# Decay attention and gated convolution on one core: first loads in halves, one more unit of 512-column value products, another hand-written order

## The chip, the cores and the metric

The kernel runs on one core of one Trainium2 chip. The metric is the device time of one execution in microseconds (us), the median of several runs. The engines are PE (TensorE, matrix products; PEld is its loading of weights), DVE (VectorE), ACT (ScalarE), POOL (GpSimd) and SP (SyncE, which here only issues transfers). All transfers go through one queue that SP feeds, onto 16 DMA engines.

## The reference

Four batches, eight heads, 768 positions and head dimension 64. A causal attention with decay and without softmax, computed block by block with a running state, is followed by a layer over 512 channels: a depthwise convolution of five taps gives a gate, a product with `w_val` gives a value, and gate times value goes through `w_out`.

```python
for b in range(nb):                       # blocks of 64 positions
    intra = einsum('bhic,bhjc->bhij', qb, kb) * Dmask      # lam ** (i - j), lower triangle
    intra = einsum('bhij,bhjd->bhid', intra, vb)
    inter = einsum('bhid,bhde->bhie', qb * lam_pow, kv_state)
    out[:, :, sl] = intra + inter
    kv_state = lam_block * kv_state + einsum('bhsd,bhse->bhde', kb * rev_pow, vb)
...
gate = sigmoid(sum_k conv_w[k] * x_shifted[k])             # five taps
result = (gate * (x @ w_val)) @ w_out
```

`w_val`, `w_out` and `conv_w` arrive as 64-bit floats.

## The kernel before

The work is cut into 12 chunks of 128 positions, each for two batches: six chunks for one pair of batches, then six for the other. For each chunk i there are, on PE, the scores `s.i` (k times q), the products `ia.i` (masked scores times v), `in.i` (q times state) and `st.i` (k times v, for the state). `ia` and `in` add up in the PSUM tile `xp`. In the first three chunks (`BIG`) the scores come in two halves, `s.i.0` into the tile `s` and `s.i.1` into `so`, and the products work on whole chunks; in the others they work on 64 x 64 tiles (`s.i.0` then holds all heads). DVE masks the scores (`m.i.b.u`, tile `A`) and updates the state (`up`); POOL scales q (`qd`) and lets the state fade (`fd`); ACT or POOL scales k (`kd`, written into the loaded tile `lv`); ACT copies `xp` away (`x`) and splits it into two float32r parts (`xh`; the low part `xl` on DVE or POOL).

Two chunks make a unit. A unit goes through the convolution (`t.un.ct.kk`, first tap on ACT, four on DVE, then `sg`, the sigmoid) and the value product with `w_val`. Each product with a weight is three matmuls (high times high, low times high, high times low), over four tiles of channels: 12 matmuls for a piece. A value piece is `v.i.f` for one chunk (256 columns) or `V.un.f` for a whole unit (512 columns), the latter for the units in `WIDE`. Gate times value is `ap`, its split `hh` and `hl`, the product with `w_out` is `p.i.b.j.u`, its copy `ev` and its store `o`. The weights are widened from 64 bits by seven small steps on DVE and ACT and one on POOL (`wv.u.k.*`, `wo.u.k.*`, `cv.*`).

SP issues loads in halves of a chunk: `ld.i.0` holds q and k with heads on partitions (tile `lq`, 1 MB), `ld.i.2` holds v and k with positions on partitions (tile `lv`, 1 MB); a half of a weight is 1 MB as well. The PSUM tile `s` has one buffer, so the scores of the next chunk wait for both masks of the chunk before.

Each engine works through its queue in order. What stands in each queue is decided by one text, `ORDER`: a list of all pieces, each with the buffers it takes after a colon. `Plan.run` walks through it and records piece after piece. The kernel begins with nine warming matmuls (`warm`), and `f.0` is one filling matmul.

Of the kernel before, what the change touches and what calls it, by code (L numbers as in the profile page):

```python
# [36 lines left out]
fd.0.0 kd.1.0 wo.1:hs1 m.1.1.1 wv.0.1.n ia.1.0:xp0 ia.1.1 wv.0.1.m:u2 ld.4.2:lv0 wv.1.0.e:val2 in.1.0 st.1:u0 wv.0.1.s
wv.0.1.w wv.0.1.v wv.0.1.h ld.3.2:lv1 wv.1.0.n s.2.0:s0 wv.1.1.e:val3 s.2.1:u1,u2 up.1.0 xh.1 wv.0.1.l v.0.1
m.2.0.0:A0 m.2.1.0 wv.1.0.m:u0 xl.1 wv.1.0.w wv.1.0.r hi.0 pb.0.0:val0 m.2.0.1:A1 wv.1.0.s cv.e qd.2.0:qd1 wv.1.0.v
qd.2.1 wv.1.1.n x.1 wv.1.1.r cv.r s.4.0:s0 cv.n v.1.0:u3 v.1.1 wv.1.0.h wv.1.1.s wv.1.1.m:u0 m.2.1.1 wv.1.1.w wv.1.1.v  # L40
ia.2.0:xp0 ia.2.1 wv.1.0.l cv.m m.4.1.0:A0 kd.2.0 wv.1.1.h fd.1.0 wo.0.0.n:val1 cv.s in.2.0 x.2:x1 pb.1.0:val2
wv.1.1.l m.4.0.0 st.2:u1 wo.0.0.e wo.0.0.r up.2.0 qd.4.0:qd0 cv.w cv.v xh.2:xs1 wo.1.1.e:val3 t.0.0.0:u2,g0 s.3.0:s0
xl.2.0 wo.0.0.m:u0 v.0.2:u3 m.3.0.0:A1 ld.6.2:lv2 v.0.3 pb.0.1 t.0.0.1 kd.3.0 t.0.0.2 xl.2.1 t.0.0.3 wo.0.0.w qd.4.1
ld.5.0:lq2 wo.0.0.s t.0.0.4 v.1.2:u1 sg.0.0 qd.3.1:qd1 v.1.3 v.2.2:u3 v.2.3 pb.1.1 wo.1.1.n fd.2.0 wo.0.0.v m.3.1.0
wo.1.1.m:u2 wo.1.1.r ld.6.0:lq0 st.3:u0,u1 wo.0.0.h qd.3.0 ia.3.0:xp0 in.3.0 wo.1.1.w wo.1.1.s wo.1.1.v wo.0.0.l hi.1
s.5.0:s0 kd.4.0 v.2.0:u2 up.3.0 in.3.1 wo.0.1.e:val1 wo.0.1.r fd.3.0 wo.1.1.h wo.0.1.n wo.0.1.m:u0 wo.0.1.s wo.1.1.l
up.3.1 fd.3.1 ia.3.1 v.2.1 x.3 xh.3 xl.3.1 ia.4.0:xp0 t.0.1.0:u1 ld.5.2:lv1 wo.0.1.w xl.3.0 pb.2.0:val3 m.5.1.0:A1
m.5.0.0 wo.0.1.v pb.2.1 wo.0.1.h wo.0.1.l s.6.0:s0 st.4:u0,u2 qd.5.1:qd1 kd.6.0 t.0.1.1 t.0.1.2 t.0.1.3 in.4.0 up.4.0
fd.4.0 t.0.1.4 sg.0.1 v.3.0:u3 kd.5.0 v.3.2:u0 qd.5.0 in.4.1 ia.4.1 ld.7.2:lv0 t.0.3.0:u1 t.0.3.1 up.4.1 t.0.3.2
x.4:x2 t.0.3.3 t.0.2.0:u2 kd.5.1 v.3.3 pb.3.1:val1 t.0.2.1 t.0.2.2 xh.4:xs0 ld.7.0:lq1 ia.5.0:xp0 in.5.0 t.0.2.3  # L50
fd.4.1 st.5:u0 up.5.0 v.3.1 pb.3.0 t.0.3.4 xl.4.1 in.5.1 sg.0.3 t.0.2.4 ap.1.0 ap.0.0 sg.0.2 ap.1.1 xl.4.0
wo.1.0.e:val2 wo.1.0.r v.4.0:u0 v.4.2:u3 wo.1.0.n wo.1.0.m:u1 ap.0.1 v.4.1 wo.1.0.s hh.1.1:hs0 wo.1.0.w pb.4.0:val0
hh.1.0 hl.1.1 wo.1.0.v m.6.1.0:A0 v.4.3 m.6.0.0 t.1.1.0:u2,g1 t.1.1.1 wo.1.0.h ia.5.1 st.6:u0,u1 up.6.0 x.5 s.7.0:s0
ia.6.0:xp0 hl.1.0 p.1.1.0.0:u0 t.1.1.2 hh.0.1:hs1 hh.0.0 t.1.1.3 pk.6 wo.1.0.l p.1.1.0.1 pb.4.1 qd.6.1:qd0 t.1.1.4
qd.6.0 t.1.3.0:u3 sg.1.1 t.1.3.1 t.1.3.2 t.1.3.3 t.1.3.4 ev.1.1.0:o0 o.1.1.0 xh.5 in.6.1 hi.2 ia.6.1 p.1.0.0.0:u2
fd.6.0 x.6:x0 t.1.0.0:u0 hl.0.0 sg.1.3 hl.0.1 p.1.0.0.1 up.6.1 ld.11.2:lv1 t.1.0.1 t.1.0.2 t.1.0.3 t.1.0.4
p.0.1.0.0:u1 ev.1.0.0:o1 p.0.1.0.1 t.1.2.0:u3 m.7.0.0:A1 t.1.2.1 t.1.2.2 t.1.2.3 m.7.1.0 sg.1.0 xl.5.0 p.0.0.0.0:u2
p.0.0.0.1 xl.5.1 v.5.0:u0 ld.8.0:lq2 t.1.2.4 ev.0.1.0:o2 o.1.0.0 xh.6:xs1 qd.7.0:qd1 t.2.3.0:u1,g0 v.5.1 ap.3.0
ld.8.2:lv2 ev.0.0.0:o0 sg.1.2 pb.5.0:val2 ap.3.1 ap.2.0 qd.7.1 kd.7.1 ia.7.0:xp0 in.7.0 kd.7.0 ap.2.1 hh.2.1:hs0
st.7:u2,u3 fd.6.1 v.5.2:u0 v.5.3 hh.2.0 t.2.3.1 t.2.3.2 up.7.0 s.8.0:s0 in.7.1 t.2.3.3 t.2.1.0:u2 t.2.3.4 hh.3.0:hs1  # L60
ia.7.1 hh.3.1 hl.2.0 sg.2.3 pb.5.1 p.2.0.0.0:u1 t.2.0.0:u0 t.2.1.1 ld.9.2:lv0 t.2.1.2 t.2.0.1 fd.7.0 up.7.1 hl.2.1
# [841 lines left out]
```

## Time and profile before

| | |
|---|---|
| median of 3 runs | 206.36 us (206.08 to 206.38) |
| profiled execution, own time | 206.52 us |
| span of its profile | 204.7 us |
| PE busy | 197.6 us, 97% of the span |
| DVE busy | 154.1 us, 75% |
| ACT, POOL busy | 114.3 and 115.4 us, 56% each |
| granted TensorE clock | 1.00 of full speed throughout |
| read, written | 29.38 MB, 6.29 MB |

The profile lists what each engine did from the start of the span; idle time carries what ended it. The own time of the profiled execution is 1.8 us longer than the span. PE is busy for nearly the whole span, so the places to read are those where PE waits and what the waiting pieces wait for.

### The profile page before, as it was taken

To read this page: it belongs to the slowest core of one execution; us is meant where nothing else is said; L and a number is where in the kernel's file an instruction comes from. 1 tells how busy PE (TensorE), PEld (TensorE's weight loads), DVE (VectorE), ACT (ScalarE), POOL (GpSimd) and SP (SyncE) were. 2 spreads that over 40 slices of the span, in tenths; PEclk is the share of its full clock that TensorE was granted. 3 is DMA by queue.
4 is the path that set the end of the run, shared out by engine and by line. 5 is a ranking of instruction groups with operands and counts; after the bars stand their busy time and mean duration, and the time that the engine had idled before them with its cause. 6 is when DMAs were issued, how large, how long until landed. Compare 5 with 4: busy or idle time off the path is not lost.

```text
span 204.7 us, 7451 instructions
## 1 busy us (share of the span) xinstructions
PE 197.6 (97%) x3312; PEld 171.6 (84%) x3312; DVE 154.1 (75%) x240; ACT 114.3 (56%) x218; POOL 115.4 (56%) x113
## 2 busy tenths in 40 slices
...
GB/s 175 426 429 419 422 424 423 421 360 27 195 51 362 8 3 118 373 232 3 297 297 29 203 400 122 3 3 152 8 106 0 0 3 102 102 51 14 93 127 78
DMA packets 7952, 36.15 MB, mean 177 GB/s; under 512 B 1136, under 2 KB 1392, under 8 KB 4336
## 3 DMA queue, kind: packets, MB, share of 16 engines
...
q14 instruction: 6, 0.05, 0.1%
HBM read 29.38 MB, written 6.29 MB: 174 GB/s over the span
## 4 chain that ended last, share of the span: by engine, by line
PE 87%; DMA 9%; SPq 2%; issue 0%; ACT 0%; ACTq 0%
PE op L841 33%; PE vp L732 33%; DMA lq<-in_qkv 9%; PE xp L510 5%; PE s L470 5%; PE xp L547 5%; PE st L572 4%; SPq L337 1%; PE xp L525 1%; PE s L460 1%; PE st L564 1%; PE xp L536 1%; SPq L355 0%; PE so L460 0%; ACT o L848 0%
## 5 line engine op out<-in xcount | busy, mean ns | idle before, releaser
L706 DVE SCALAR_TENSOR_TENSOR acc<-x,conv_sb,acc 128x512 f32<-128x512 f32 x96 | 71.5, 753 | 7.8 <-ACT acc L704 5.7
L732 PE MATMUL vp<-x_hi,wv_hi 128*128 128x256 f32 (+1 forms) x144 | 47.1, 327 | 0.0
L732 PE MATMUL vp<-x_hi,wv_lo 128*128 128x256 f32 (+1 forms) x144 | 45.9, 319 | 0.3 <-POOL wv_lo L303 0.3
L732 PE MATMUL vp<-x_lo,wv_hi 128*128 128x256 f32 (+1 forms) x144 | 45.8, 318 | 0.0
L841 PE MATMUL op<-wo_hi,hs 128*128 128x512 f32 x96 | 30.4, 398 | 0.0
L848 ACT COPY o<-op 128x512 f32<-128x512 f32 (+1 forms) x25 | 14.3, 570 | 28.5 <-PE op L841 24.2
L732 PEld LDWEIGHTS vp<-x_hi,wv_hi 128*128 128x128 f32 x144 | 27.3, 190 | 2.8
L732 PEld LDWEIGHTS vp<-x_hi,wv_lo 128*128 128x128 f32 x144 | 27.4, 190 | 2.4 <-POOL wv_lo L303 0.5
L732 PEld LDWEIGHTS vp<-x_lo,wv_hi 128*128 128x128 f32 x144 | 27.4, 190 | 1.9
L677 POOL TENSOR_TENSOR x_lo<-x,x_hi 128x512 fp32r<-128x512 f32 x20 | 25.8, 1311 | 4.7 <-ACT x_hi L666 4.7
L584 POOL TENSOR_TENSOR sdec<-state,qdec_c 128x512 f32<-128x512 f32 x17 | 18.4, 1080 | 9.2 <-DVE state L581 9.2
L814 POOL TENSOR_TENSOR hs<-g,hs 128x512 fp32r<-128x512 f32 x12 | 15.4, 1294 | 13.6 <-ACT hs L803 13.6
L420 POOL TENSOR_TENSOR qd<-lq,qdec_c 128x512 f32<-128x512 f32 (+1 forms) x18 | 22.6, 1272 | 0.0
L841 PEld LDWEIGHTS op<-wo_hi,hs 128*128 128x128 f32 x96 | 17.7, 188 | 4.0
L841 PE MATMUL op<-wo_hi,h_hi 128*128 128x512 f32 (+1 forms) x52 | 20.0, 385 | 0.0
L841 PE MATMUL op<-wo_hi,h_lo 128*128 128x512 f32 (+1 forms) x52 | 19.6, 377 | 0.0
L704 ACT ACTIVATE acc<-x,conv_sb 128x512 f32<-128x512 f32 x24 | 16.7, 696 | 5.1 <-DVE state L581 3.6
L841 PE MATMUL op<-wo_lo,h_hi 128*128 128x512 f32 (+1 forms) x52 | 19.5, 375 | 0.0
L841 PE MATMUL op<-wo_lo,hs 128*128 128x512 f32 x48 | 18.9, 393 | 0.0
L803 ACT CAST h_hi<-vp 128x512 fp32r<-128x512 f32 x12 | 6.9, 587 | 21.0 <-DVE vp L778 21.0
L581 DVE TENSOR_TENSOR state<-st,sdec 128x512 f32<-128x512 f32 x17 | 11.7, 688 | 8.8 <-PE xp L547 6.4
L778 DVE TENSOR_TENSOR vp<-vp,g 128x512 f32<-128x512 f32 x12 | 8.3, 698 | 11.9 <-PE vp L732 11.9
...
## 6 DMA issues: line engine op xcount, KB each, us to landing
...
lam_bc<-in_lam SPq DMA_DIRECT2D x1, 4.0 KB, 1.6
```

What stands on the lines that cost most here:

```text
L420: nc.gpsimd.tensor_tensor(out=s["qd"][:, hs, ms], in0=lds[i]["qT"][:, u].rearrange("p h (m i) -> p h m i", m=2)[:, :, ms], in1=qdec[:, hs, ...
L470: nc.tensor.matmul(sp[b][rows(m), k, :], t["kT"][rows(b), u, h, ms], t["qT"][rows(b), u, h, ms], start=True, stop=True,)
L510: nc.tensor.matmul(s["xp"][rows(hh), b ^ m, b, g, :], lds[i]["v"][rows(m), b, h * D : (h + 1) * D], s["A"][rows(m), b, h, :], start=b == 0 ...
L581: nc.vector.tensor_tensor(out=state, in0=s["st"][m], in1=sdec, op=ALU.add)
L584: nc.gpsimd.tensor_tensor(out=sdec, in0=state, in1=qdec_c[:, :, n - 1 : n].to_broadcast([P, H, D]), op=ALU.mult)
L677: nc.gpsimd.tensor_tensor(out=s["x_lo"][:, ts], in0=s["x"][:, ts], in1=s["x_hi"][:, ts].bitcast(F32), op=ALU.subtract)
L704: nc.scalar.mul(to, src, w)
L706: nc.vector.scalar_tensor_tensor(out=to, in0=src, scalar=w, in1=to, op0=ALU.mult, op1=ALU.add)
L732: nc.tensor.matmul(to, w[:, ct, fs], xx[:, ct], start=n_mm == 0, stop=n_mm == 3 * NT - 1)
L814: (nc.vector if direct else nc.gpsimd).tensor_tensor(out=to, in0=x["h", j, fs], in1=x["to", j, fs].bitcast(F32), op=ALU.subtract)
L841: nc.tensor.matmul(s["op", b, j][:, cols], hh, w[:, ft, cols], start=ft == 0 and n == 0, stop=ft == NT - 1 and n == 2,)
L848: nc.scalar.copy(s["o", b, j][:, cols], s["op", b, j][:, cols])
```

## The change

Four things change. The first q and k load comes in two halves by head group (`ld.0.0`, `ld.0.1`, 0.5 MB each), and the first MB of `w_val` in two halves as well (`wv.0.0`, `wv.0.1`). Unit 2 (chunks 4 and 5) joins `WIDE`, so that its value products have 512 columns. `ORDER` is written anew from the first line to the last.

```diff
-WIDE = (3,4,5)
+WIDE = (2,3,4,5)
+SPLIT = (("wv", 0),)
 ORDER = """
-ld.0.0:lq0 dm.0 dm.1 qe ld.0.2:lv0 kd.0.0 s.0.0:s0 kd.0.1 m.0.0.0:A0 s.0.1:u0,u1 m.0.1.0 ia.0.0:xp0 wv.0:g0 ld.1.0:lq1
...
+qe dm.0 ld.0.0:lq0 s.0.0:s0 wv.0.0:g0 f.0:u0 cv dm.1 ld.0.1 s.0.1:u0,u1 ld.0.2:lv0 kd.0.1 cv.e wv.0.0.n:val0 wv.0.0.e
...
+            def tile_of(i=i, lo=lo, tag=tag):
+                if (i, lo) not in ld_tile:
+                    t = ld_tile[i, lo] = buf(tag, tag, [P, 2, 2, DM])
...
+                return ld_tile[i, lo]
+
+            for part in ((0, 1), (1, 2)) if (i, lo) == (0, 0) else ((0, 2),):
+
+                def go(lo=lo, part=part, tile_of=tile_of, src=qkv[pair, c]):
+                    nc.sync.dma_start(tile_of()[:, slice(*part)], src[:, lo + part[0] : lo + part[1]])
+
+                t = add(f"ld.{i}.{lo + part[0]}", "DMA", go, [], [ld_buf[i, lo]])
+                for q in range(*part):
+                    t_ld[i, lo + q] = t
...
-                def go(u=u, got=got):
-                    t = buf(home, "w_raw", [P, 4 * DM], I32)
-                    nc.sync.dma_start(t, src[u].bitcast(I32))
-                    got[u] = t.rearrange("p (n two) -> p n two", two=2)
-
-                t_go = add(f"{name}.{u}", "DMA", go, [], [b])
+                def go(lo, hi, u=u, got=got):
+                    if u not in got:
+                        got["raw"] = buf(home, "w_raw", [P, 4 * DM], I32)
+                        got[u] = got["raw"].rearrange("p (n two) -> p n two", two=2)
+                    ws = slice(2 * DM * lo, 2 * DM * hi)
+                    nc.sync.dma_start(got["raw"][:, ws], src[u].bitcast(I32)[:, ws])
+
+                t_go = {}
+                for lo, hi in ((0, 1), (1, 2)) if (name, u) in SPLIT else ((0, 2),):
+                    t = add(f"{name}.{u}" + (f".{lo}" if hi - lo == 1 else ""), "DMA", lambda lo=lo, hi=hi, go=go: go(lo, hi), [], [b])
+                    for k in range(lo, hi):
+                        t_go[k] = t
```

The first place is SP's queue at the start of the program. Before, it begins so (`lq` and `lv` are the two loads of a chunk, `w_raw` a half of a weight, 2048 columns are 1 MB):

```order
L174 DMA lam_bc<-in_lam 128x8
L337 DMA lq<-in_qkv 128x2048
L337 DMA lv<-in_qkv 128x2048
L355 DMA w_raw<-in_w_val 128x2048
L337 DMA lq<-in_qkv 128x2048
L337 DMA lv<-in_qkv 128x2048
L355 DMA w_raw<-in_w_val 128x2048
L337 DMA lq<-in_qkv 128x2048 x2
L370 DMA conv_raw<-in_conv_w 128x40
```

And after the change:

```order
L175 DMA lam_bc<-in_lam 128x8
L344 DMA lq<-in_qkv 128x1024
L365 DMA w_raw<-in_w_val 128x1024
L383 DMA conv_raw<-in_conv_w 128x40
L344 DMA lq<-in_qkv 128x1024
L344 DMA lv<-in_qkv 128x2048
L365 DMA w_raw<-in_w_val 128x1024
L344 DMA lq<-in_qkv 128x2048
L344 DMA lv<-in_qkv 128x2048
L365 DMA w_raw<-in_w_val 128x2048
L344 DMA lq<-in_qkv 128x2048 x2
```

The first v load now has 1.5 MB ahead of it where it had 1 MB, and the convolution weights have moved from the ninth place to the fourth. Everything from the second `lq` (chunk 1) on stands behind the same 3 MB as before, plus the 20 KB of the convolution weights.

The second place is PE's queue from the state product of chunk 0 (`st`) to the scores of chunk 4 (`s`, 64x64). Before, with the twelve matmuls of a value piece (`vp`, 128x256) cut to the first two:

```order
L564 MATMUL st<-lv 64x64 x16
L460 MATMUL s<-lq 128x128 x8
L460 MATMUL so<-lq 128x128 x8
L732 MATMUL vp<-x_hi,wv_hi 128x256
...
L525 MATMUL xp<-A,lv 64x128 x16
L536 MATMUL xp<-qd,state 64x128 x16
L564 MATMUL st<-lv 64x64 x16
L460 MATMUL s<-lq 128x128 x8
L460 MATMUL so<-lq 128x128 x8
L732 MATMUL vp<-x_hi,wv_hi 128x256
...
L470 MATMUL s<-lq 64x64 x32
```

And after the change:

```order
L577 MATMUL st<-lv 64x64 x16
L473 MATMUL s<-lq 128x128 x8
L473 MATMUL so<-lq 128x128 x8
L538 MATMUL xp<-A,lv 64x128 x16
L549 MATMUL xp<-qd,state 64x128 x16
L577 MATMUL st<-lv 64x64 x16
L745 MATMUL vp<-x_hi,wv_hi 128x256
...
L473 MATMUL s<-lq 128x128 x8
L473 MATMUL so<-lq 128x128 x8
L483 MATMUL s<-lq 64x64 x32
```

The first value piece `v.0.0` stood between the scores of chunk 1 and the first use of chunk 1's v (`xp<-A,lv`); it now stands behind chunk 1's state product. The second, `v.0.1`, stood between the scores of chunk 2 and those of chunk 4; the two sets of scores now follow each other directly.

## Rows read from the trace of the kernel before

**Rows 1.** The page: busy time, share of the span and instructions.
```profile
PE 197.6 (97%) x3312; PEld 171.6 (84%) x3312; DVE 154.1 (75%) x240; ACT 114.3 (56%) x218; POOL 115.4 (56%) x113
```

**Rows 2.** PE's waits: who for whom, us in total, times, longest.
```profile
PE s L460 <- DMA lq<-in_qkv: 1.9, 3, 0.9
PE warm L188 <- DVE zero L179: 1.1, 1, 1.1
PE xp L525 <- DVE A L483: 0.5, 1, 0.5
PE vp L732 <- POOL wv_lo L303: 0.3, 1, 0.3
```

**Rows 3.** Timeline of PE, 0 to 24 us: start, length, instruction, idle before.
```profile
1.05 4.21 PE L188 MATMUL warm<-zero 128*128 128x128 f32 x18 [1.05 <-DVE zero L179]
6.21 1.16 PE L460 MATMUL s<-lq 64*128 64x128 f32 x16 [0.95 <-DMA lq<-in_qkv]
...
13.64 1.16 PE L460 MATMUL s<-lq 64*128 64x128 f32 x16 [0.45 <-DMA lq<-in_qkv]
...
15.62 0.39 PE L732 MATMUL vp<-x_hi,wv_hi 128*128 128x256 f32 x1
...
17.85 1.97 PE L525 MATMUL xp<-A,lv 128*64 128x128 f32 x32
19.75 1.10 PE L536 MATMUL xp<-qd,state 64*64 64x128 f32 x32
20.78 1.15 PE L564 MATMUL st<-lv 128*64 128x64 f32 x32
22.45 1.16 PE L460 MATMUL s<-lq 64*128 64x128 f32 x16 [0.52 <-DMA lq<-in_qkv]
```

**Rows 4.** Timeline of ACT at the scaling of chunk 1's k.
```profile
17.71 2.45 ACT L401 ACTIVATE lv<-lv,mask_c 128x128 f32<-128x128 f32 x8 [0.42 <-DMA lv<-in_qkv]
```

**Rows 5.** Timeline of DVE at the masks of chunk 2's first half.
```profile
23.66 1.29 DVE L483 TENSOR_TENSOR A<-s,mask_c 128x512 f32<-128x512 f32 x2
```

**Rows 6.** DMA queues, 15 to 16 us: packets, MB, share of 16 engines.
```profile
q1 hardware_dynamic: 63, 0.39, 93.5%
q8 instruction: 1, 0.02, 5.5%
```

**Rows 7.** DMA queues, 22 to 23 us, the convolution weights among them.
```profile
q1 hardware_dynamic: 165, 0.40, 100.4%
```

**Rows 8.** The chain that ended last: start, us, what.
```profile
24.51 1.62 PE vp L732 x12
...
48.81 0.62 PE xp L547 x32
49.43 0.47 PE xp L510 x32
49.90 1.63 PE vp L732 x12
...
55.08 3.06 PE vp L732 x24
...
86.62 2.85 PE vp L732 x24
...
154.85 10.89 PE vp L732 x48
...
201.75 0.37 ACT o L848
```

**Rows 9.** Windows: busy us of PE, PEld, DVE, ACT, POOL; clock; DMA share; GB/s.
```profile
10.00:15.00 5.00, 4.40 (x72) 3.29 (x72) 3.68 (x8) 3.38 (x7) 2.12 (x2) 1.00 1.02 433
15.00:20.00 5.00, 4.66 (x66) 4.03 (x66) 3.98 (x9) 4.55 (x13) 3.56 (x4) 1.00 1.00 419
...
25.00:30.00 5.00, 5.00 (x97) 4.80 (x96) 5.00 (x11) 3.80 (x10) 2.52 (x3) 1.00 1.00 424
30.00:35.00 5.00, 5.00 (x151) 4.46 (x152) 4.97 (x9) 4.53 (x13) 3.96 (x4) 1.00 1.01 423
...
40.00:60.00 20.00, 19.90 (x603) 18.88 (x602) 17.03 (x25) 17.42 (x43) 17.66 (x16) 1.00 0.45 170
```

**Rows 10.** The costliest groups of DVE: count, busy us, mean ns.
```profile
L706 DVE SCALAR_TENSOR_TENSOR acc<-x,conv_sb,acc 128x512 f32<-128x512 f32 x96 | 71.5, 753 | 7.8 <-ACT acc L704 5.7
...
L778 DVE TENSOR_TENSOR g<-val,g 128x512 f32<-128x512 f32 x12 | 7.8, 687 | 1.1 <-ACT g L711 1.1
```

More of the change, by code (lines that the diff above doesn't have):

```diff
@@ L37 @@
[L37 to L61, printed above, removed]
@@ new lines @@
+wv.0.1.r wv.0.0.l m.1.0.0 ia.1.0:xp0 ld.3.2:lv0 m.1.0.1:A1 m.1.1.1 ld.3.0:lq1 fd.0.0 ia.1.1 wv.0.1.m:u2 wv.0.1.w
+kd.1.0 wv.0.1.s wv.0.1.v wv.1.0.e:val2 wv.1.0.r wv.1.0.n wv.1.0.m:u3 wv.1.1.e:val3 wv.0.1.h in.1.0 x.1 st.1:u0
+v.0.0:u1 wv.1.1.n wv.1.0.s hi.0 wv.1.1.r ld.5.2:lv1 wv.1.0.w wv.1.0.v wv.0.1.l s.2.0:s0 m.2.0.0:A0 qd.2.1:qd1 m.2.1.0
+up.1.0 xh.1 xl.1 qd.2.0 fd.1.0 s.2.1:u2,u3 m.2.0.1:A1 wv.1.1.m:u0 m.2.1.1 wv.1.1.w wv.1.0.h wv.1.0.l kd.2.0 s.4.0:s0
+v.0.1 wv.1.1.s wo.0.1.e:val0 wo.0.1.r wo.0.0.n:val1 wv.1.1.v ia.2.0:xp0 ia.2.1 wo.0.1.n in.2.0 wo.0.0.e st.2:u2
@@ new lines @@
+kd.9.0 qd.10.0:qd0 V.3.3:u3 fd.8.1 ev.3.1.0:o0 sg.3.0 t.3.1.1 t.3.1.2 t.3.1.3 kd.9.1 t.3.1.4 o.3.1.0 ld.10.2:lv2
+ia.9.0:xp0 st.9:u2,u1 in.9.0 up.9.0 apw.2.3 sg.3.1 ld.11.0:lq2 t.3.2.0:u0 xh.8:xs0 s.10.0:s0 t.3.2.1 t.3.2.2 hi.4
+fd.9.0 qd.10.1 in.9.1 V.3.0:u2 up.9.1 V.3.1:u1 t.3.2.3 t.3.2.4 fd.9.1 m.10.1.0:A0 sg.3.2 V.3.2:u0 kd.10.0 apw.3.3
+hhw.3.3:hs1 m.10.0.0 apw.3.0 hhw.3.0 ia.9.1 s.11.0:s0 apw.3.1 xl.8.0 kd.10.1 apw.2.1 hhw.3.1 x.9 hlw.3.1:val2
+hlw.3.3:val0 st.10:u1,u3 hhw.2.1:hs0 apw.3.2 hlw.3.0 ia.10.0:xp0 in.10.0 apw.2.2 p.7.0.0.0:u2 hhw.3.2 hlw.3.2
```

93 lines of the change are left out of this document (51 added, 42 removed).

## The prediction

> **What bounds the kernel now.** The page first: PE is busy 97% of the span, DVE 75% [rows 1]. Then PE's waits. There are only four entries, 3.8 us together, and the largest, 1.9 us in three waits, is for q loads [rows 2]. The timeline puts all of them in the first 22.45 us: the three waits for q loads come before the scores of chunks 0, 1 and 2 [rows 3]. From 22.45 us on the chain of work that ended last is PE, piece after piece, until the last copy of 0.37 us on ACT [rows 8]. So the time is: the moment at which chunk 2's scores can start, plus all PE work that is then left, plus a short tail. The change can move the end by starting chunk 2's scores at another moment with the same work done, by making PE's remaining work shorter, or by putting new holes into it.
>
> **The start.** Before, the first scores start at 6.21 us, 0.95 us after the warming matmuls, because the whole MB must land [rows 3]. With half a MB they can start when the warming ends, near 5.26 us. This gain is lost at once: the second half of the scores waits for the load that stands third (behind half a MB of `w_val`), and the first v load stands behind 1.5 MB instead of 1 MB. Chunk 1's scores come at 13.64 us with a wait of 0.45 us for their load [rows 3], and that load stands behind the same 3 MB as before. The early gain therefore buys nothing as long as chunk 0's products are done before 13.6 us. They are, by a chain of durations: v at about 9.9 us (2.5 MB at the roughly 2.5 us per MB that lie between the loads at 6.21 and 13.64 us, three MB apart), two sets of `ia` about 2.1 us, `st` about 1.2 us: near 13.3 us.
>
> Two extra loads and the convolution weights now go ahead. In the microsecond in which the convolution weights pass, the queue moved 0.40 MB with its engines full [rows 7], against 433 GB/s and 419 GB/s over five microseconds [rows 9], so 20 KB in small packets costs at most 0.05 us. The price of halving a load is not in the trace; the bounds are nothing (the queue is never empty here) and a whole step of 2.5 us for each half. I take 0.0 because the engines work through packets and always have the next load's behind them, and I add 0.05 us for the weights.
>
> **Chunk 1, the term that decides.** Chunk 1's v is the load after chunk 1's q. At the pace above it would land near 16.1 us. ACT got it at 17.71 us after waiting 0.42 us [rows 4]. The queue moved 419 GB/s all the while [rows 9], so the bytes didn't slow down; what is special in that stretch is one packet of PE's instructions, which took 5.5% of 16 engines for a microsecond, 0.88 us of one engine [rows 6]. A load counts as landed when all 16 engines have done their share, so one engine that serves instructions makes the load late. That is my inference; the delay of 1.6 us is a fact.
>
> Before, PE filled that hole with `v.0.0`, from 15.62 to 17.85 us, and then ran `ia`, `in` and `st` of chunk 1 from 17.85 to 21.93 us. It waited 0.52 us for chunk 2's q load and started its scores at 22.45 us [rows 3]. In the new order `v.0.0` stands behind `st`. The hole after chunk 1's scores stays empty, and `ia` can't start before 17.71 us plus the 0.05 us and PE's own latency, so about 17.9 us. PE then needs the same 4.08 us and the 1.63 us of a value piece that stands between attention pieces [rows 8]: 17.9 + 4.08 + 1.63 = 23.6 us. Chunk 2's scores start about 1.15 us later with the same work done (1.63 less the 0.52 that was idle, plus 0.05).
>
> **A new wait behind chunk 2's scores.** Chunk 4's scores use the one buffer of tile `s`, so they wait for both masks of chunk 2's first half. DVE started these 1.21 us after the scores began (23.66 against 22.45 us) and took 1.29 us [rows 3, 5]: 2.50 us. PE's two halves of chunk 2's scores take 2.06 us, from 22.45 to the value piece at 24.51 us [rows 3, 8]. That piece, 1.62 us, stood in between and hid the wait; now it stands behind. PE idles 2.50 - 2.06 = about 0.45 us. All that is queued on PE is late by as much. The bounds are 0 (if DVE were quicker, which no row shows) and 1.0 us (if DVE is itself behind).
>
> **What gets shorter.** Unit 2's products: 96 matmuls of 256 columns become 48 of 512. In a run without attention pieces ahead, 24 took 2.85 us, 118.8 ns each; 48 of 512 columns took 10.89 us, 226.9 ns each [rows 8]. 96 x 118.8 - 48 x 226.9 = 11.40 - 10.89 = 0.5 us. The Trainium skill (TensorE: Matmul & The Clock Gate, "Wait — 56ns, not 53.3ns?") gives columns over 2.4 GHz plus a fixed 2.5 ns for each matmul; by that rule the saving would be 48 x 2.5 ns, an estimate of 0.12 us. The rows give four times as much, 0.5 us over 48 matmuls saved or 10.7 ns each, and the sum goes by the rows.
>
> Fewer turns between kinds of work. 24 value matmuls behind attention took 3.06 us against 2.85 us, so entering costs 0.21 us; an attention piece right behind value products took 0.62 us against 0.47 us for its neighbour, so leaving costs 0.15 us [rows 8]. Counted in the two orders, PE goes from attention pieces to value or output products 22 times before and 20 times after. Two pairs less give 2 x 0.36 = 0.7 us.
>
> The other work is the same: conv taps, masks, splits and POOL's steps keep their number, the narrow copies of unit 2 only take another shape, and the last piece is still an output product of 256 columns with its copy and store.
>
> **Sum.** +1.15 + 0.45 - 0.5 - 0.7 = +0.4 us. On the profiled execution's own 206.52 us that is 206.9 us; the median of the runs shown lies 0.16 us under it, so 206.75 us. This measurement tells about 0.2% from no change, 0.41 us: 205.95 to 206.77 us counts as the same. My forecast is no change, at the upper edge. Its own range is 206.2 to 207.3 us.
>
> **The rivals.**
>
> *The instruction packet misses chunk 1's v.* If it comes a little later against the load, or on an engine that is through with its share, v lands near 16.1 us. Then DVE's masks set the start: the first half of chunk 1's scores ends near 14.85 us, and a mask, the state update and the other mask, three steps of 0.645 us (half of the 1.29 us of two) [rows 5], end at an estimated 16.8 us. `st` ends near 20.9, `v.0.0` near 22.6 us, close to the landing of chunk 2's q. The 1.15 us shrink to about 0.15 us, and the time is 205.75 us, faster. For it: only one such packet stands in this stretch, and its moment is not the loads' own. Against it: both the load and PE's place in its instructions hang on chunk 1's q load, and PE has as many instructions ahead of it as before.
>
> *DVE becomes the bound in the first third.* DVE was full from 25 to 35 us and had 3 us free from 40 to 60 [rows 9]. Ahead of `ia.5.0` the new order has 92 DVE pieces, the old one 82: three taps at 0.75, four gate products at 0.69 [rows 10] and three weight steps of about 0.6 us more, 6.8 us, while PE has one value piece more ahead of it. The new order gives back some 1.7 us by widening `w_val` in DVE's early idle time, and PE's 1.6 us delay gives the rest of the room: 6.8 against 1.7 + 3 + 1.6 = 6.3 us. From half a microsecond of extra waiting on DVE there, PE waits for its masks and state updates. I price it at 1 us: 207.75 us, slower. Against it: not every piece listed ahead is needed by PE there.
>
> *The halves are slow.* If half a load takes the step of a whole one, two steps of half of 2.5 us are added ahead of chunk 1, and everything is 2.4 us later: 209.1 us. The Trainium skill (DMA: Bandwidth & Descriptors, "Bandwidth") has a rule for it: batch transfers to at least 1 MiB for at least 75% of peak. The rows speak against it here, since 20 KB in small packets passed almost for nothing [rows 7].
>
> **How the numbers follow.** Chances: forecast 0.45, packet misses 0.28, DVE bound 0.23, slow halves 0.04. Faster: 0.21 of the second and 0.07 of the first, 0.28. Slower: 0.13 of the first, 0.20 of the third, 0.04 of the last, 0.37. Same: 0.35. The range leaves out the slow halves, the worse half of the DVE case and the best of the second: 205.4 to 207.8 us.
>
> **What would show it.** The first scores near 5.3 us; chunk 1's `ia` behind a hole of about 2 us that ends on the v load near 17.9 us; chunk 2's scores near 23.6 us without a wait for their load; chunk 4's scores with a wait of about 0.45 us on DVE's masks; PE without further waits of note to the end; a chain with two turns less. I am wrong if v lands near 16 us, if PE waits on DVE between 25 and 65 us, or if the unit-2 products save another amount than 0.5 us.

## The result, and the profile after

The changed kernel takes 208.86 us (median of 4 runs, 208.55 to 208.99), beside 206.37 us before (206.08 to 206.46): the ratio is 1.0118, with a 95% interval of 1.0103 to 1.0133. It is slower by 2.5 us, 2.1 us over the forecast and outside its range. (Medians here and below are of all executions; a ratio leaves out those that took over 1.5% more than the quickest of the same kernel.) The profiled execution took 208.73 us, its span is 207.0 us.

The page of after; the line answers to [rows 1]:

```profile
PE 196.7 (95%) x3264; PEld 170.0 (82%) x3264; DVE 152.4 (74%) x240; ACT 115.1 (56%) x218; POOL 115.0 (56%) x113
```

PE has 0.9 us less to do and is busy for a smaller share of a longer span: the time was lost in holes. PE's waits of after (who for whom, us in total, times, longest), which answer to [rows 2]:

```profile
PE so L473 <- DMA lq<-in_qkv: 2.1, 1, 2.1
PE xp L538 <- DVE A L496: 1.6, 1, 1.6
PE xp L538 <- DMA lv<-in_qkv: 1.2, 1, 1.2
...
PE s L483 <- PE so L473: 0.5, 1, 0.5
...
PE xp L560 <- DVE state L594: 0.3, 1, 0.3
```

Three holes are new: the second half of chunk 0's scores waits 2.1 us for its half load, chunk 0's `ia` 1.2 us for v, chunk 1's `ia` 1.6 us for DVE's masks. The timeline of PE (start, length, instruction, idle before) shows where they are; it answers to [rows 3]:

```profile
5.60 1.16 PE L473 MATMUL s<-lq 64*128 64x128 f32 x16 [0.34 <-DMA lq<-in_qkv]
...
9.89 1.16 PE L473 MATMUL so<-lq 64*128 64x128 f32 x16 [2.08 <-DMA lq<-in_qkv]
12.30 3.55 PE L538 MATMUL xp<-A,lv 128*64 128x128 f32 x32 [1.25 <-DMA lv<-in_qkv]
...
20.33 1.97 PE L538 MATMUL xp<-A,lv 128*64 128x128 f32 x32 [1.56 <-DVE A L496]
...
25.97 1.16 PE L473 MATMUL s<-lq 64*128 64x128 f32 x16
```

Chunk 2's scores start at 25.97 us. Before it was 22.45 us [rows 3]; the forecast said 23.6. Between them and the end of PE's last product the trace of after has 177.88 us (25.97 to 203.85), that of before 179.24 (22.45 to 201.69). So the change loses 3.5 us at the start and gains 1.4 us behind it.

The chain of after at the start says what each step waited for (start, us, what):

```profile
3.05 9.12 DMA lv<-in_qkv
...
12.30 3.57 PE xp L538 x32
...
15.89 1.08 ACT x_hi L677 x2
...
16.99 1.29 DVE x_lo L685 x2
18.28 0.60 DVE A L496
18.88 0.60 DVE state L592
19.48 0.61 DVE A L496
...
20.33 1.97 PE xp L538 x32
```

The reader is to see two things. The v load of chunk 0 lands at 12.16 us, where the forecast had 9.9. And chunk 1's `ia` at 20.33 us hangs on the queue of DVE, which does `x_lo` of chunk 0, a mask, the state and a mask one after another, and not on chunk 1's v load as forecast. The windows of after (busy us of the engines, then PE's clock, DMA share, GB/s) give the reason for the late v load, and one for the late DVE:

```profile
3.00:4.00 1.00, 1.00 (x7) 1.00 (x7) 1.00 (x4) 0.00 (x0) 0.76 (x4) 1.00 0.91 229
4.00:5.00 1.00, 1.00 (x6) 0.96 (x5) 1.00 (x3) 0.00 (x0) 0.92 (x2) 1.00 0.91 225
5.00:6.00 1.00, 0.66 (x8) 0.40 (x8) 1.00 (x2) 0.00 (x0) 0.92 (x2) 1.00 0.90 201
6.00:7.00 1.00, 1.00 (x15) 0.86 (x14) 0.46 (x1) 0.00 (x0) 0.18 (x1) 1.00 0.91 248
...
12.00:13.00 1.00, 0.70 (x7) 0.73 (x9) 1.00 (x2) 0.22 (x1) 0.70 (x1) 0.59 1.02 422
13.00:14.00 1.00, 1.00 (x12) 1.00 (x11) 0.96 (x3) 0.00 (x0) 1.00 (x2) 0.50 1.01 422
14.00:15.00 1.00, 1.00 (x14) 1.00 (x12) 1.00 (x3) 0.00 (x0) 0.38 (x1) 0.50 1.05 442
```

From 3 to 7 us the DMA engines are about 90% busy, and yet the queue moves 201 to 248 GB/s. Before, the same four microseconds had 311, 401, 385 and 426 GB/s. Over 2 to 9 us 0.66 MB less came through, 1.6 us at 420 GB/s. And from 12 to 15 us the granted clock is near 0.50, the lower level of 1.2 GHz: PE had been idle for 2.1 and 1.3 us just before, and `ia` of chunk 0 takes 3.55 us instead of the 1.97 us of another chunk [rows 3]. The time doesn't show it, though: of the four executions two had a mean granted clock of 1.000 and took 208.55 and 208.99 us, the other two had 0.990 and 0.991 and took 208.99 and 208.73 us.

The landings say more than the windows. The loads of chunk 1 are issued at 4.13 us (q and k) and 4.79 us (v and k); the last number is the time from issue to landing in us:

```profile
lq<-in_qkv SPq DMA_DIRECT2D x1, 1024.0 KB, 12.1
lv<-in_qkv SPq DMA_DIRECT2D x1, 1024.0 KB, 13.9
```

They land at 16.2 and 18.7 us, 2.5 us apart. Before, the same loads were issued at 2.57 and 3.32 us and landed 11.0 and 14.4 us later, at 13.6 and 17.7 us, 4.1 us apart, which agrees with the waits that end there [rows 3, 4]. So chunk 1's q is 2.6 us late and its v only 1.0 us: the extra 1.6 us of v, which the forecast carried over from before, are not in this execution.

### The profile page after: what moved, and what is told of

Its sections match the earlier page's. It is cut to its first block, busy times and chain, and to the rows that moved or that the text cites. A ratio compares the mean times of both kernels' runs of the same rounds, so it can differ in the third digit from the quotient of the medians.

```text
span 207.0 us, 7367 instructions
## 1 busy us (share of the span) xinstructions
PE 196.7 (95%) x3264; PEld 170.0 (82%) x3264; DVE 152.4 (74%) x240; ACT 115.1 (56%) x218; POOL 115.0 (56%) x113
## 4 chain that ended last, share of the span: by engine, by line
PE 90%; DMA 4%; DVE 2%; SPq 1%; issue 1%; ACT 1%; ACTq 0%; DVEq 0%
PE vp L745 33%; PE op L854 33%; PE xp L560 5%; PE xp L523 5%; DMA lv<-in_qkv 4%; PE st L585 4%; PE s L483 4%; PE xp L538 4%; PE st L577 1%; PE xp L549 1%; DVE x_lo L685 1%; DVE A L496 1%; PE s L473 1%; ACT x_hi L677 1%; PE so L473 0%
## 5 line engine op out<-in xcount | busy, mean ns | idle before, releaser
L745 PEld LDWEIGHTS vp<-x_hi,wv_hi 128*128 128x128 f32 x128 | 24.2, 189 | 3.2
L745 PEld LDWEIGHTS vp<-x_hi,wv_lo 128*128 128x128 f32 x128 | 24.3, 190 | 2.5
L854 PE MATMUL op<-wo_hi,h_hi 128*128 128x512 f32 (+1 forms) x68 | 26.2, 386 | 0.0
L854 PE MATMUL op<-wo_hi,h_lo 128*128 128x512 f32 (+1 forms) x68 | 25.8, 380 | 0.0
L854 PE MATMUL op<-wo_lo,h_hi 128*128 128x512 f32 (+1 forms) x68 | 25.6, 377 | 0.0
L724 ACT ACTIVATE g<-acc 128x512 f32<-128x512 f32 x24 | 14.3, 599 | 20.4 <-DVE acc L719 20.3
L854 PE MATMUL op<-wo_hi,hs 128*128 128x512 f32 x64 | 20.2, 397 | 0.0
L647 ACT COPY x<-xp 128x512 f32<-128x512 f32 x24 | 12.9, 591 | 9.5 <-PE xp L523 8.6
L827 POOL TENSOR_TENSOR hs<-g,hs 128x512 fp32r<-128x512 f32 x8 | 10.5, 1313 | 9.7 <-ACT hs L816 9.7
L854 PEld LDWEIGHTS op<-wo_lo,h_hi 128*128 128x128 f32 x68 | 12.9, 190 | 2.5
```

The costliest lines, as they stand in the source:

```text
L647: nc.scalar.copy(*blocks(s["x"], b))
L724: nc.scalar.activation(xu[un]["g"][:, ct].rearrange("p u (b i) -> p b u i", b=NB2), xu[un]["acc", ct].rearrange("p b (u i) -> p b u i", u= ...
L745: nc.tensor.matmul(to, w[:, ct, fs], xx[:, ct], start=n_mm == 0, stop=n_mm == 3 * NT - 1)
L827: (nc.vector if direct else nc.gpsimd).tensor_tensor(out=to, in0=x["h", j, fs], in1=x["to", j, fs].bitcast(F32), op=ALU.subtract)
L854: nc.tensor.matmul(s["op", b, j][:, cols], hh, w[:, ft, cols], start=ft == 0 and n == 0, stop=ft == NT - 1 and n == 2,)
```

## The experiments

The names beginning with b are changes of the kernel before, those with a of the changed kernel, hyb takes the start of before and the rest of the new order. Times are medians, ratios are to the kernel before on the same chip.

**What a split load costs: b_qhalf, b_whalf, b_wsep, b_quart, b_wpart.** On the kernel before, with its order, only one load is split.

```diff
@@ b_qhalf @@
-ld.0.0:lq0 dm.0 dm.1 qe ld.0.2:lv0
+ld.0.0:lq0 ld.0.1 dm.0 dm.1 qe ld.0.2:lv0
@@ b_whalf @@
-ia.0.0:xp0 wv.0:g0 ld.1.0:lq1
+ia.0.0:xp0 wv.0.0:g0 wv.0.1 ld.1.0:lq1
@@ b_wsep @@
+ia.0.0:xp0 wv.0.0:g0 ld.1.0:lq1 wv.0.1
@@ b_quart @@
+ia.0.0:xp0 wv.0.0:g0 wv.0.0b wv.0.1 wv.0.1b ld.1.0:lq1
@@ b_wpart, with the order of b_whalf @@
-nc.sync.dma_start(got["raw"][:, ws], src[u].bitcast(I32)[:, ws])
+pp = slice(P // 2 * lo, P // 2 * hi)
+nc.sync.dma_start(got["raw"][pp], src[u].bitcast(I32)[pp])
```

> The kernel before, with nothing changed but the first q and k load, which comes in two halves one right behind the other; every byte stands where it stood. Theory (packets of 4 KB take as long as those of 8 KB in the first microseconds of the queue): chunk 0's v lands about 1 us later than in the kernel before, all later loads as well, chunk 2's scores start near 23.4 us instead of 22.45 us, and the time is about 207.3 us. Rival (halves move at full rate, the late loads of the changed kernel come from their order): chunk 2's scores at 22.5 us and 206.4 us.

> The kernel before, with only the first MB of w_val in two halves, at its old third place in the queue, where it moves between 8.7 and 11.2 us. Theory (only the queue's first microseconds are slow for small packets): no later load, 206.4 us. Rival (halves of w_val are slow wherever they stand): the loads behind come about 1.2 us later, chunk 2's scores near 23.6 us, 207.6 us.

> b_whalf with chunk 1's q load (1 MB, 8 KB packets) between the two halves of w_val's first MB. Theory (half loads are slow only beside each other): no hole below 400 GB/s from 6 to 14 us, and the time is that of before, 206.5 us, but for what the earlier q load changes. Rival (each half load is slow wherever it stands): two holes near 300 GB/s, 207 us.

> The kernel before with the first MB of w_val in four loads by columns (2 KB packets), third in the queue. Halving it cost a hole of 0.7 us in the queue and 0.5 us of time. Theory (each extra load costs that much): a hole of about 2 us from 8 to 12 us, 207.6 us or more. Rival (the price comes once, with the change of the packets' size): a hole of 0.7 us, 207.1 us.

> The kernel before with the first MB of w_val in two loads by partitions (64 partitions each, 8 KB of a row in one packet) in place of two loads by columns (128 partitions, 4 KB), third in the queue. Theory (the 4 KB packets of neighbouring half loads are what is slow): the queue stays near 420 GB/s from 8 to 10 us and the time is that of before, 206.5 us. Rival (a second load of half the size costs by itself, whatever its packets): a hole as with columns, about 300 GB/s from 8 to 10 us, 207.1 us.

Measured: b_qhalf 207.34 us, ratio 1.0040 (1.0025 to 1.0055); b_whalf 207.07, 1.0030 (1.0017 to 1.0042); b_wsep 209.02, 1.0130 (1.0087 to 1.0173); b_quart 208.10, 1.0084 (1.0069 to 1.0099); b_wpart 209.10, 1.0131 (1.0090 to 1.0172). The windows at the place of the split load, of b_qhalf, then b_whalf, b_quart and b_wpart (GB/s stand last; the kernel before has 311 and 401, and then 410, 418, 426 and 442):

```profile
3.00:4.00 1.00, 1.00 (x7) 1.00 (x7) 1.00 (x4) 0.00 (x0) 0.76 (x4) 1.00 0.84 127
4.00:5.00 1.00, 0.84 (x6) 0.65 (x5) 1.00 (x3) 0.00 (x0) 0.92 (x2) 1.00 0.87 258
```

```profile
8.00:9.00 1.00, 0.53 (x12) 0.36 (x8) 1.00 (x3) 0.00 (x0) 0.01 (x1) 1.00 0.99 311
9.00:10.00 1.00, 1.00 (x19) 1.00 (x20) 1.00 (x2) 0.00 (x0) 1.00 (x1) 1.00 0.97 233
```

```profile
8.00:9.00 1.00, 0.64 (x12) 0.45 (x8) 1.00 (x3) 0.00 (x0) 0.00 (x0) 1.00 0.91 182
9.00:10.00 1.00, 0.90 (x16) 0.93 (x18) 1.00 (x3) 0.00 (x0) 0.89 (x1) 1.00 0.87 135
10.00:11.00 1.00, 1.00 (x20) 0.81 (x16) 0.28 (x1) 0.00 (x0) 1.00 (x2) 1.00 1.03 383
```

```profile
9.00:10.00 1.00, 0.14 (x3) 0.17 (x5) 1.00 (x2) 0.00 (x0) 0.14 (x1) 1.00 1.04 213
...
13.00:14.00 1.00, 0.97 (x32) 1.00 (x32) 0.00 (x0) 0.00 (x0) 0.00 (x0) 1.00 0.88 229
14.00:15.00 1.00, 0.18 (x7) 0.04 (x2) 0.52 (x2) 0.06 (x1) 0.00 (x0) 1.00 0.99 418
```

The DMA engines are 84% busy or more in each hole, so it is the packets that take longer, not the queue that is empty. Against the windows of before the hole is 0.8 us for the halved q load (0.34 MB at 420 GB/s, 2 to 6 us), 0.7 us for the halved weight (0.28 MB), 1.3 us for quarters (0.55 MB, 8 to 11 us). The times are longer by 0.8, 0.5 and 1.8 us. So a split load costs more the finer it is split; the hole grows less than in proportion. The theory of b_qhalf holds (chunk 2's scores at 23.49 us); that of b_whalf falls, since the hole comes at 8 us too; b_quart's hole lies between its theory and its rival. The loads behind a split land later than the hole is long: in b_qhalf chunk 0's v at 10.2 us instead of 8.6 and chunk 1's q at 15.1 instead of 13.6, in b_whalf chunk 1's q at 14.4. Why is not shown. The 2.5 us that were my upper bound for a half were too much, and my 0.0 too little.

b_wsep has the hole as well (320 and 258 GB/s from 8 to 10 us), where its first half stands alone, so neighbouring halves are not the reason: that theory falls. Its rival falls too, for the second half has no hole: it moves from 12 to 14 us, at 389 and 430 GB/s. (Its time is longer for another reason: the second half now lands behind 1 MB more, DVE's widening waits for it in its order, and PE waits 2.1 us for the weights.)

b_wpart was to tell whether 4 KB packets are the cause, and can't: with 8 KB packets into 64 partitions the queue runs at about 220 GB/s for 5 us, half its speed, so these loads are slow for a reason of their own. Loads that fill only half the partitions are worse than loads of half the columns. What settles the question is the packets of b_wsep from 12 to 13 us and of b_quart from 10 to 11 us:

```profile
DMA packets 98, 0.39 MB, mean 389 GB/s; under 512 B 16, under 2 KB 16, under 8 KB 85
DMA packets 213, 0.38 MB, mean 383 GB/s; under 512 B 26, under 2 KB 26, under 8 KB 213
```

Nearly all of them are under 8 KB, and the queue is at nine tenths of its pace. So small packets as such are not slow. Slow are the first two microseconds of a split (four in the changed kernel, where three half loads come close together), and why stays open. The Trainium skill (DMA: Bandwidth & Descriptors, "Bandwidth") says to batch to at least 1 MiB for at least 75% of peak. The first halves agree in direction, at 127 to 311 GB/s; the second half of b_wsep, 0.5 MB at 389 and 430 GB/s, does not.

**The change with the q load whole: a_qwhole, a_qwhole2 (once more), a_qs4.**

```diff
@@ a_qwhole, a_qwhole2 @@
-qe dm.0 ld.0.0:lq0 s.0.0:s0 wv.0.0:g0 f.0:u0 cv dm.1 ld.0.1 s.0.1:u0,u1
+qe dm.0 ld.0.0:lq0 s.0.0:s0 wv.0.0:g0 f.0:u0 cv dm.1 s.0.1:u0,u1
-            for part in ((0, 1), (1, 2)) if (i, lo) == (0, 0) else ((0, 2),):
+            for part in ((0, 2),):
@@ a_qs4, on a_qwhole @@
-kd.2.0 s.4.0:s0 v.0.1 wv.1.1.s
+kd.2.0 v.0.1 s.4.0:s0 wv.1.1.s
```

> The changed kernel with the first q and k load whole again, in its first place; w_val's first MB stays in halves, which now stand apart (half, weights of the convolution, v, half). Order of every engine as changed. Theory (neighbouring half loads are slow, and that made chunk 0's v 2.2 us late): v lands near 10 us, ia.0 starts near 10.2 us, chunk 1's v load then sets ia.1 near 17.9 us, chunk 2's scores near 23.6 us, 206.5 us. Rival (DVE's order ahead of ia.1 sets it whatever the loads do): ia.1 not before 20 us, 208.6 us or more.

> a_qwhole once more, for a profile of an execution with the full clock (the first one had the half clock in ia.1). Theory: chunk 0's v near 11 us, ia.1 of 2.0 us behind chunk 1's v at 18 to 18.9 us, chunk 2's scores near 24.2 us, own time 206.3 to 207.0 us. Rival (something other than the clock made those runs shorter): ia.1 of 2.0 us, but an own time over 208 us.

> a_qwhole with chunk 4's scores behind v.0.1, as before the change: the 0.5 us for which they wait for chunk 2's masks is then covered. Theory: 0.5 us less than a_qwhole beside it, 206.3 us where a_qwhole has 206.8. Rival (ia.2 then waits for chunk 2's other masks on DVE, which end 1.2 us behind): the same time as a_qwhole.

Measured: in 10 of the 21 executions of a_qwhole and a_qwhole2 the mean clock was 0.997 to 1.000, and they took 206.15 to 207.04 us, ratio 1.0020 (1.0007 to 1.0032) for those of a_qwhole; in the other 11 the clock was 0.98 to 0.99 and the time 208.5 to 211.6 us. The changed kernel's executions at full clock took 208.55 and 208.99 us. So at full clock this one undone split is worth 2.1 us, and what is left of the change lands where the forecast had it, at no difference from before. Both profiled executions had the lower clock, so no trace shows a quick one. The timeline of PE in a_qwhole2:

```profile
11.08 2.19 PE L538 MATMUL xp<-A,lv 128*64 128x128 f32 x32 [0.95 <-DMA lv<-in_qkv]
...
18.76 3.43 PE L538 MATMUL xp<-A,lv 128*64 128x128 f32 x32 [2.06 <-DMA lv<-in_qkv]
...
26.01 1.16 PE L473 MATMUL s<-lq 64*128 64x128 f32 x16
```

Chunk 0's `ia` starts at 11.08 us instead of 12.30, and chunk 1's v load decides when its `ia` starts, as the forecast said, though at 18.76 us. There the granted clock fell to 0.50 behind 2.06 us of idle PE, which costs 1.5 us (3.43 against 1.97). That explains the execution of 208.54 us (less 1.5 us it is one of the quick ones), but not those of 210.5 us and more; what they lose besides stays open. The agreement of the quick ones with the forecast is partly luck: less these 1.5 us chunk 2's scores would start near 24.5 us, 0.9 us behind the forecast's 23.6, and the chain behind them is shorter than forecast (below).

a_qs4 took 208.48 us, ratio 1.0109 (1.0071 to 1.0148). The wait of chunk 4's scores is gone, and from chunk 2's scores to chunk 2's `ia` PE needs 4.91 us (23.75 to 28.66) instead of 5.32 (26.01 to 31.33): 0.4 us, the size forecast. The time isn't shorter than that of a_qwhole's quick executions. In the profiled execution, of 207.84 us, PE stands still for 1.35 us later; the chain:

```profile
40.18 0.62 PE xp L523 x31
40.80 1.35 issue
42.15 0.27 PE xp L523
```

Nor is the clock all that tells executions apart: one of a_qs4 took 209.29 us at a mean clock of 1.000.

**PE kept busy: a_again (the changed kernel once more), a_fill, a_fill2, a_qfill.** Filling matmuls in PE's holes are to keep the clock up and change nothing else.

```diff
@@ a_fill @@
-f.0:u0 cv dm.1 ld.0.1 s.0.1:u0,u1 ld.0.2:lv0
+f.0:u0 f.1:u3 f.2:u3 cv dm.1 ld.0.1 s.0.1:u0,u1 f.3:u3 ld.0.2:lv0
@@ a_fill2 @@
+f.0:u0 f.1:u3 cv dm.1 ld.0.1 s.0.1:u0,u1 f.2:u3 ld.0.2:lv0
@@ a_qfill, on a_qwhole @@
-s.1.1:u0,u1 x.0:x0
+s.1.1:u0,u1 f.1:u2 f.2:u2 x.0:x0
```

> The changed kernel once more, beside the others on the same chip: 208.9 us. If the profiled execution has the full clock from 12 to 16 us, ia.0 takes 2.0 instead of 3.55 us; theory (the half clock costs 1.1 to 1.5 us): 207.5 us; rival (the next wait, for chunk 1's q load or DVE's masks, takes it up): 208.6 us or more.

> The changed kernel with three more filling matmuls on PE, two while it waits for the second half of the scores and one while it waits for chunk 0's v. Theory (PE's granted clock fell to half because PE idled 2.1 and 1.25 us there, and chunk 0's products then took 3.55 us instead of 2.06): the clock stays at full, these products take about 2.06 us, chunk 2's scores start 1.5 us earlier, 24.5 us instead of 26.0, and the time is about 207.4 us. Rival (the slow stretch is hidden behind DVE and the loads): the products are fast and the time stays at 208.8 us.

> The changed kernel with two filling matmuls more behind f.0 and two behind the second half of chunk 0's scores, short enough not to delay what follows (the four of a_fill ran past the landing of the second half of q and k). They keep PE busy from 7.8 to 9 us and from 11 to 12.1 us. Theory (the half clock in ia.0 comes from PE's idle time, and costs about 1 us): full clock from 12 to 16 us, ia.0 2.0 us long, chunk 2's scores near 25 us, 207.9 us. Rival (DVE's order takes it up): full clock, but 208.6 us or more.

> a_qwhole with four filling matmuls in the 2.2 us for which PE waits ahead of ia.1; all else as there, where six of eleven runs had a clock below full speed and took 209.5 to 211.5 us, the other five 206.3 to 207.0 us. Theory (PE's idle time lowers the clock in those runs, and the half clock costs 3 us or more): full clock in all runs, 206.7 us. Rival (the clock falls for another reason): again two groups of times.

Measured: a_again 209.55 us, ratio 1.0141 (1.0110 to 1.0172), with a mean clock of 0.984 to 0.992 in all runs; a_fill 213.06, 1.0219 (1.0162 to 1.0276); a_fill2 209.61, 1.0167 (1.0128 to 1.0207); a_qfill 209.04, 1.0113 (1.0075 to 1.0152). In a_fill the matmuls ran past the landing of the second half, which made everything behind late: it tells nothing of the clock. a_fill2 does:

```profile
12.13 1.97 PE L538 MATMUL xp<-A,lv 128*64 128x128 f32 x32 [0.20 <-DMA lv<-in_qkv]
...
19.23 1.97 PE L538 MATMUL xp<-A,lv 128*64 128x128 f32 x32 [1.40 <-DMA lv<-in_qkv]
...
24.87 1.16 PE L473 MATMUL s<-lq 64*128 64x128 f32 x16
```

At full clock chunk 1's `ia` waits for its v load again, and chunk 2's scores start 1.1 us earlier than in the changed kernel. So the clock and the DVE chain behind it cost 1.1 us there, and the late loads the other 1.3 us of the 2.4 over the forecast (24.87 against 23.6). But the time isn't shorter: in this profile PE stands still for 0.38 us near 42 us and 0.81 us near 101 us without a wait for any engine. The theory was right on the start, the rival on the time: all four executions of a_fill2 had a mean clock of 0.999 or 1.000, and none was quicker than the changed kernel's 208.86 us. So the clock is not what made the change slower. a_qfill still has two of four runs at a lower clock, so the hole ahead of chunk 1's products isn't the only place where the clock falls; and its two at full clock took 208.03 and 208.40 us, over 1 us more than the quick ones of a_qwhole. In its profile PE stands still for 0.87 us near 100 us.

**The hole filled with work: a_v00, a_qv00.** `v.0.0` goes back in front of `ia.1.0` and is gone behind `st.1`, on the changed kernel and on a_qwhole.

```diff
@@ a_v00; from there on u1 and u3 change names @@
-wv.0.0.l m.1.0.0 ia.1.0:xp0
+wv.0.0.l m.1.0.0 v.0.0:u3 ia.1.0:xp0
@@ a_qv00, on a_qwhole; u1 and u3 change names as in a_v00 @@
-m.0.1.1 kd.0.0 qd.1.0:qd0 qd.1.1 ld.4.0:lq0
+m.0.1.1 kd.0.0 ld.4.0:lq0
...
-xh.0:xs0 wv.0.1.e:val1 wv.0.0.h cv.w
+xh.0:xs0 wv.0.0.h wv.0.0.l qd.1.0:qd0 qd.1.1 wv.0.1.e:val1 cv.w
...
-wv.0.0.l m.1.0.0 ia.1.0:xp0
+m.1.0.0 v.0.0:u3 ia.1.0:xp0
```

> The changed kernel with the first value piece of chunk 0 back in the hole ahead of chunk 1's first products with v, where the kernel before has it (another PSUM buffer is taken so that it can start there). Theory (the hole of 1.6 us in front of those products is wasted, and the piece then costs its full 1.63 us behind chunk 1's state product): chunk 2's scores start near 24.4 us instead of 26.0 and the time is about 207.2 us. Rival (the piece waits for the low part of chunk 0's x, done at 18.3 us, ends after 20.3 us and pushes chunk 1's products): 0.3 to 0.6 us less gain, 207.7 us; or, if chunk 2's q load is what ends last, nothing beyond its landing near 24.1 us.

> a_qwhole with v.0.0 ahead of ia.1.0 (in the hole before chunk 1's v), and POOL's low part of the first weight tile ahead of chunk 1's qd, so that v.0.0 doesn't wait for it. Theory (the hole's 1.6 us come back and PE has no idle time that lowers its clock): chunk 2's scores near 23.1 us, 205.9 us in all runs. Rival (POOL's or DVE's order makes v.0.0 late and it pushes ia.1 back): 206.7 us or more.

Measured: a_v00 210.70 us, ratio 1.0219 (1.0183 to 1.0256); a_qv00 207.76, 1.0064 (1.0045 to 1.0083). In a_v00 the value products wait 0.8 us for POOL's low part of the weights, and `ia.1` starts at 21.11 us, later than in the changed kernel (20.33). In a_qv00 chunk 2's scores start at 23.13 us, exactly as expected, and the mean clock is below 0.998 in one run only (0.99); then PE stands still for 0.26 us at 26.91 and for 1.00 us at 40.99 us. That is most of the 1.9 us by which a_qv00 misses its theory, and neither theory nor rival had it. For a_v00 the rival named the late value products, but not the size; PE stands still for 0.25 us near 43 us there, and where the rest is lost isn't shown.

**The start of before with the rest of the new order: a_whole, hyb2, hyb3, hyb4.** a_whole takes the new order with whole loads, and the widening of the first weights behind chunk 0's masks. hyb2 to hyb4 take the order of before up to chunk 2's products.

```diff
@@ a_whole @@
-qe dm.0 ld.0.0:lq0 s.0.0:s0 wv.0.0:g0 f.0:u0 cv dm.1 ld.0.1 s.0.1:u0,u1 ld.0.2:lv0 kd.0.1 cv.e wv.0.0.n:val0 wv.0.0.e
+qe dm.0 ld.0.0:lq0 s.0.0:s0 f.0:u0 cv dm.1 s.0.1:u0,u1 ld.0.2:lv0 kd.0.1 cv.e
...
+m.0.1.0 wv.0:g0 ld.1.0:lq1
...
+m.0.1.1 wv.0.0.n:val0 wv.0.0.e wv.0.0.r wv.0.0.s
@@ hyb2, where the two orders meet @@
+wo.0.1.e:val0 wo.0.1.r wo.0.0.n:val1 ia.2.0:xp0 ia.2.1 wo.0.1.n in.2.0 wo.0.0.e st.2:u1
...
+up.2.0 xl.2.0 v.1.0:u0 v.1.1
@@ hyb3; hyb4 has v.1.0:u2 @@
+wo.0.1.e:val0 wo.0.1.r wo.0.0.n:val1 v.1.0:u0 v.1.1 ia.2.0:xp0 ia.2.1 wo.0.1.n in.2.0 wo.0.0.e st.2:u1
```

> The changed kernel with both loads whole again (first q and k load first, then the convolution weights, v, the MB of w_val, as before); the widening steps of the first MB stand behind chunk 0's masks on DVE. Everything else is the new order. Theory (the halves' late landings cost most of the 3.5 us): chunk 0's v at about 10 us instead of 12.2, chunk 1's v sets ia.1 near 17.9 us, chunk 2's scores near 23.6 us, and the time is 208.9 - 2.3 = 206.5 us. Rival (the order of DVE's steps ahead of ia.1 costs it, and the halves only a little): chunk 2's scores not before 25 us, 207.9 us or more.

> The order of before up to chunk 2's products (whole loads), the new order from there on, with 512 columns in unit 2; chunk 2's four masks stand together on DVE. Theory (the new order behind chunk 2's scores has 1.4 us less on PE's path, 177.9 against 179.2 us, or 1.9 us without the wait of chunk 4's scores; only the start lost it): 204.5 to 205.0 us. Rival (the later part gained because PE ran 3.5 us late and DVE had had time to get ahead): 206.0 to 207 us, with PE waits for DVE between 25 and 65 us.

> hyb2 with chunk 1's value products back in front of ia.2.0, where they stood before: they cover chunk 1's copy and chunk 2's masks on DVE, for which ia.2.0 waited 1.3 us in hyb2. Theory (the start of before and the rest of the new order add up): 206.8 - 1.3 - 0.7 (st.2 took 1.8 instead of 1.1 us behind that wait) = 204.8 us, faster than both kernels. Rival (DVE is behind by then, and the wait only moves to ia.3 or to the value products): 206 us or more.

> hyb3 with another PSUM buffer for chunk 1's value products: in hyb3 they took the one that the weight steps of the second MB still held, and PE waited 4.8 us. The start is that of before, the rest the new order. Theory (the new order behind chunk 2's scores is shorter by 1.4 us, 1.9 without the wait of chunk 4's scores, and only the start lost it): 204.5 to 205.0 us. Rival (the later part is quick only when DVE is ahead by PE's late start): 206 us or more, with PE waits for DVE between 25 and 65 us.

Measured: a_whole 213.09 us, ratio 1.0327 (1.0270 to 1.0384); hyb2 206.83, 1.0015 (1.0003 to 1.0026); hyb3 213.36, 1.0330 (1.0294 to 1.0365); hyb4 206.78, 1.0020 (1.0011 to 1.0030). a_whole failed as a test: the moved widening steps kept DVE until 23.7 us, PE waited 6.2 us for its masks, and its first products ran at the slower level. In hyb2 chunk 2's `ia` waits 1.3 us for the copy of chunk 1 on ACT. In hyb3 the value products meant to cover that took a buffer that steps of the weights still held, and PE waits 4.8 us. hyb4 is the clean one, and its theory falls: with chunk 2's scores at 22.39 us PE needs 179.48 us to the end, as before (179.24), not 177.9. Its chain shows one that holds PE up:

```profile
22.20 14.93 DMA lv<-in_qkv
...
37.31 3.79 POOL qd L433 x3
...
41.15 0.46 PE xp L560 x16
```

A v load that SP issued at 22.20 us lands at 37.12 us, POOL comes late with its qd, PE waits. It is one of three waits behind chunk 2's scores, two of which are for other engines (us, times, longest):

```profile
PE xp L560 <- POOL qd L433: 0.6, 1, 0.6
PE vp L745 <- DVE state L594: 0.5, 1, 0.5
```

With one of 0.4 us inside PE's own queue they are 1.5 us, and without them the 179.48 us would be 178.0, the theory's 177.9. So PE's work is shorter, and from an early start loads, POOL and DVE take the gain back. In the changed kernel PE comes 3.5 us later and has only the waits of 0.5 and 0.3 us above. No version was faster than before.

## Why the prediction was wrong

**The step that failed** is the price of the halves: "I take 0.0 because the engines work through packets and always have the next load's behind them". The queue was never empty, that part holds; but a halved load ran at 0.4 to 0.8 of the speed before for two microseconds. Measured on the kernel before it is 0.8 us for q and 0.7 us for `w_val`, in the changed kernel 1.6 us for both together, and the loads land still later than that: chunk 0's v came at 12.16 us and not at 9.9, chunk 1's q at 16.2 and not at 13.6. My row for it was a small load of 20 KB that passed among whole ones [rows 7], and it did not answer the question. I gave this case 0.04. Its 2.4 us of lateness fit chunk 1's q (2.6 us); that its time, 209.1 us, is so near the measured one is partly luck, since chunk 1's v was only 1.0 us late and what follows made up the rest.

**What followed from the late v.** PE stood idle twice, and its clock fell to the lower level for chunk 0's `ia`. The early gain wasn't just lost at once: it moved PE's idle time to where the clock fell, which made the start later in the profiled execution, though the times at full clock are no shorter. DVE then had `x_lo`, two masks and the state to do in its order, and chunk 1's `ia` started at 20.33 us. The forecast had 17.9 us and the v load as the last to come; that v had landed at 18.7 us. That load decides it again (18.76 and 19.23 us) as soon as the q load is whole or the clock stays up, 0.9 to 1.3 us later than I had it.

**What held.** The hole of chunk 1 is not filled by `v.0.0`, and the 1.63 us behind `st` come on top. Chunk 4's scores wait 0.49 us (forecast 0.45); a_qs4 takes the wait away and wins 0.4 us at that place. Unit 2's products take 10.9 us instead of 11.4 on the chain, outside the piece's entries: 0.5 us, as the rows said. By the 2.5 ns per matmul of the Trainium skill (TensorE: Matmul & The Clock Gate, "Wait — 56ns, not 53.3ns?") it would have been an estimated 0.12 us.

**What was mis-sized.** The turns: forecast -0.7 us. The chain behind chunk 2's scores is shorter by 1.36 us although it has 0.5 us more of the wait above and 0.3 us of a wait for the state; so about 2.1 us are saved, 0.5 of them in unit 2, 1.6 in turns and pieces like them. I counted two pairs, and where the rest comes from wasn't isolated. hyb4 shows that this gain was not to be had with the early start of before.

**The rivals.** DVE as the bound from 25 to 65 us did not come: besides the forecast 0.5 us PE's only later wait for DVE is 0.3 us. The first rival came true in its first half: chunk 1's v was not held back in the changed kernel, and the next load, the second MB of `w_val`, lands 3.0 us behind it, at 21.7 us. The instruction packet stands at 18 us there. In hyb4, which loads as the kernel before does, v lands at 16.2 us, 2.4 us behind chunk 1's q; in a_qwhole2 it is 4.1 us behind again. So these 1.6 us come and go, and a sum should not have carried them over as fixed; that the packet causes them is still only argued. The rival's gain did not come, because q was late and DVE's masks came last.
